# Channel mixing on one core: the first product by Strassen's scheme for four of six token blocks, with the weights' parts kept in DRAM

## The chip, the cores and the metric

The kernel runs on one core of a Trainium2 chip, in float32 values from end to end, where each value that a matmul takes is cut into two fp32r parts. The metric is the device time of one execution in microseconds (us). A profile of one execution is read beside it. Its engines are PE (TensorE, the matmuls), DVE (VectorE), ACT (ScalarE), POOL (GpSimd) and SP (which issues the DMAs here).

## The reference, cut to what matters

Three layers follow one another: attention with pooled queries, a mixture of four small attention experts, and a mixer. The change lies in the last lines, the channel mixing.

```python
def _moe2_ref(x, U, V, w_ch1, w_ch2):
    xt = x.transpose(0, 2, 1)
    h = xt @ U @ V
    u = x + h.transpose(0, 2, 1)                       # 4 x 576 x 512
    ch = np.maximum(u @ w_ch1, 0.0) @ w_ch2            # 512 -> 2048 -> 512
    return (u + ch).astype(np.float32)
```

## The kernel before, in words

The first 730 us belong to attention, the experts and the token mixing; they leave `u` in DRAM (`u_d`, 2304 tokens of 512 features). Channel mixing then takes six **token blocks** x of 384 tokens. The 2048 hidden features are 16 **slices** fi of 128. A slice has a tile `w` with its part of both weights, each of them as a high and a low half in fp32r.

For one block and one slice, `mlp(x, fi)` does this. `up` runs 12 matmuls of 128x384 into a PSUM bank `ms` (L1096): four chunks of 128 features, and for each high times high, high times low, low times high. ACT writes `hh`, the ReLU in fp32r (L1099), and DVE writes what is left over, `hl` (L1100). `down` runs 9 matmuls of 128x512 into the block's three banks `o` (L1107), and is called one step late: the `down` of the step before stands behind the `up` of this one, so that ACT and DVE have the length of a `down` for `hh` and `hl`. I call one such step a **tick**.

Slices go in `NG = 4` groups of `FG = 4`: within a group all six blocks are done, each over the group's four slices, and then DVE adds `o` to the block's `u` (`close_block`, L1112, three adds). There are 24 such closings. The order is `order = [(x, fi) for g ... for x ... for fi ...]`. Block 0 with the first group runs already among the experts' work (`CM`).

Weights arrive as float64. `weights` loads one tile of 128x512 as pairs of int32 (`raw`, 512 KB). `decode_steps` makes float32 of them in six DVE instructions (L241 to L246, tiles `dca` and `dcb`), and `cut` splits the result: ACT copies the high half (L224), and DVE, or POOL for the first group, subtracts it for the low half (L225). Of the 32 tiles the first eight are made during the experts' work. The other 24 are made by `ahead`, half a tile per tick, over three of the four groups.

`turn` transposes a block's `u`: three PE transposes (L1088) into a bank `ms`, then `cut` into `uh` and `ul`. The order of the instructions on PE, DVE and ACT is written out by hand:

```python
        if pend:
            finish()
        pend.append((x, fi, hl, ob[x]))
```

PSUM has three banks for `ms`, and the `o` of an odd block takes one of them (`OB`).

## Time and profile before

| | before |
|---|---|
| time, median of 3 runs | 1136.07 us (1135.33 to 1137.54) |
| profiled execution, its own time | 1135.58 us |
| span of that execution in the profile | 1133.6 us |
| PE busy over the span | 1099.6 us (97%) |
| DVE, ACT, POOL busy | 753.6, 456.1, 499.9 us |
| read from DRAM, written | 52.65 MB, 9.44 MB |

The profile is of one execution, whose own time is 1.98 us over its span. Busy shares are means over the whole span; the stage of the change is its last 400 us, where POOL has nothing to do and PE hardly ever waits.

### The profile page before, as it was taken

The numbers are of one execution on the slowest core, as the hardware profiler recorded it, in microseconds if no ns is written. First come the engines' busy times: TensorE is split into PE (matmuls) and PEld (weight loads), VectorE is DVE, ScalarE is ACT, GpSimd is POOL, SyncE is SP. The second block draws the span as 40 slices with busy tenths as digits, with TensorE's granted clock in tenths as the row PEclk, the third lists the DMA queues.
The fourth block names the chain that finished last, engine by engine and source line by source line (L and its number), as shares of the span: only waits on it lengthen the run. The fifth ranks groups of instructions, "written<-read, shape, count | busy, mean of one in ns | idle before, by whom it ended". The sixth has DMA issues, their size and how long they took to land.

```text
span 1133.6 us, 18983 instructions
## 1 busy us (share of the span) xinstructions
PE 1099.6 (97%) x6748; PEld 905.9 (80%) x6748; DVE 753.6 (66%) x1625; ACT 456.1 (40%) x1173; POOL 499.9 (44%) x492
## 2 busy tenths in 40 slices
...
POOL 6788999888888889844243334200000000000000
...
GB/s 143 193 177 187 183 199 173 170 175 198 176 173 157 179 142 90 43 43 43 43 43 85 38 170 103 143 129 56 57 19 32 61 56 1 56 56 5 53 56 56
DMA packets 115118, 117.96 MB, mean 104 GB/s; under 512 B 70352, under 2 KB 86736, under 8 KB 115024
## 3 DMA queue, kind: packets, MB, share of 16 engines
...
q8 instruction: 53, 0.87, 0.3%
q14 instruction: 41, 0.34, 0.1%
HBM read 52.65 MB, written 9.44 MB: 55 GB/s over the span
## 4 chain that ended last, share of the span: by engine, by line
PE 87%; DVE 7%; ACT 2%; issue 1%; DMA 1%; POOL 0%; POOLq 0%; ACTq 0%; SPq 0%
PE ms L1096 17%; PE o L1107 17%; PE pv L624 12%; PE ms L743 9%; PE st L604 8%; PE ms L556 7%; PE st L605 6%; PE pv L894 2%; PE ms L631 2%; DVE mp L558 2%; PE ms L504 1%; PE ms L815 1%; PE st L870 1%; PE st L869 1%; PE pv L946 1%
## 5 line engine op out<-in xcount | busy, mean ns | idle before, releaser
L616 POOL TENSOR_TENSOR acc<-acc,pt 128x576 f32<-128x576 f32 x224 | 319.5, 1427 | 34.0 <-ACT pt L606 19.5
L606 ACT ACTIVATE pt<-st 128x288 f32<-128x288 f32 x576 | 219.6, 409 | 187.8 <-PE st L605 140.7
L558 DVE TENSOR_REDUCE mp<-ms 128x1 f32<-128x384 f32 x432 | 215.1, 549 | 57.5 <-PE ms L556 55.5
L1096 PE MATMUL ms<-uh,w 128*128 128x384 f32 x768 | 214.4, 340 | 1.0 <-DVE ul L225 1.0
L1107 PE MATMUL o<-w,hh 128*128 128x512 f32 x576 | 180.9, 395 | 2.5 <-ACT hh L1099 2.2
L1100 DVE SCALAR_TENSOR_TENSOR hl<-ms,hh 128x384 fp32r<-128x384 f32 x96 | 53.5, 558 | 186.4 <-ACT hh L1099 185.9
L1099 ACT ACTIVATE hh<-ms 128x384 fp32r<-128x384 f32 x96 | 47.2, 491 | 273.7 <-PE ms L1096 273.7
L624 PE MATMUL pv<-pt,vr 128*64 128x288 f32 x1152 | 153.9, 412 | 0.0
L556 PE MATMUL ms<-kn,bd 128*128 128x384 f32 x432 | 146.3, 365 | 3.3 <-DVE mp L558 1.5
L1096 PEld LDWEIGHTS ms<-uh,w 128*128 128x128 f32 x768 | 141.0, 188 | 4.9 <-DVE ul L225 0.9
L1096 PE MATMUL ms<-ul,w 128*128 128x384 f32 x384 | 130.1, 339 | 0.7 <-DVE ul L225 0.7
L624 PEld LDWEIGHTS pv<-pt,vr 128*64 128x64 f32 x1152 | 80.8, 138 | 56.3 <-issue 5.2
L1107 PEld LDWEIGHTS o<-w,hh 128*128 128x128 f32 x576 | 107.0, 188 | 20.5 <-ACT hh L1099 2.5
L1107 PE MATMUL o<-w,hl 128*128 128x512 f32 x288 | 113.6, 394 | 0.0
L604 PE MATMUL st<-q1a,s1a 128*128 128x288 f32 x288 | 93.6, 325 | 2.2 <-ACT pt L606 2.0
L604 PE MATMUL st<-q1b,s1b 128*128 128x288 f32 x288 | 92.5, 321 | 0.2 <-ACT pt L606 0.2
L556 PEld LDWEIGHTS ms<-kn,bd 128*128 128x128 f32 x432 | 81.0, 194 | 14.0 <-DVE mp L558 5.8
L605 PE MATMUL st<-q2a,s2a 128*128 128x288 f32 x288 | 85.3, 296 | 0.0
L605 PE MATMUL st<-q2b,s2b 128*128 128x288 f32 x288 | 85.0, 295 | 0.0
L1096 PEld LDWEIGHTS ms<-ul,w 128*128 128x128 f32 x384 | 72.2, 188 | 5.3 <-DVE ul L225 1.9
L604 PEld LDWEIGHTS st<-q1a,s1a 128*128 128x128 f32 x288 | 54.4, 189 | 24.7 <-issue 21.2
L886 POOL TENSOR_TENSOR acc<-acc,pt 128x576 f32<-128x576 f32 (+4 forms) x48 | 45.9, 956 | 50.2 <-ACT pt L877 48.3
...
## 6 DMA issues: line engine op xcount, KB each, us to landing
...
```

The source lines that it names most:

```text
L556: nc.tensor.matmul(ps[:, :384], BD[i % 2][:, t, :], KN[i % 2][:, c * 384:c * 384 + 384], start=True, stop=True)
L558: nc.vector.tensor_reduce(st["mp"][:, t, c:c + 1], ps[:, :384], axis=X, op=ALU.max)
L604: nc.tensor.matmul(ps[:, :HT], pr.S1[a][:, ks], pr.Q1[a][:, qs], start=True, stop=False)
L605: nc.tensor.matmul(ps[:, :HT], pr.S2[a][:, ks], pr.Q2[a][:, qs], start=False, stop=True)
L606: nc.scalar.activation(c["pt"][:, a, :], ps[:, :HT], AF.Exp, scale=0.0625)
L616: nc.gpsimd.tensor_add(acc[i, h], acc[i, h], c["pt"])
L624: nc.tensor.matmul(o[64 * a:64 * a + 64, :HT], vr[:, a, kt, :], c["pt"][:, a, :], start=(kt == 0), stop=(kt == NKT - 1))
L743: nc.tensor.matmul(ps, stat[x][s], mov[x][m], start=(x == 0 and y == 0), stop=(x == n - 1 and y == 2))
L1096: nc.tensor.matmul(ps[:, :TB], W[fi][:, 0, a, cs], m[:, c, :], start=(c == 0 and y == 0), stop=(c == NC - 1 and y == 2))
L1099: nc.scalar.activation(h, ps[:, :TB], AF.Relu)
L1100: nc.vector.scalar_tensor_tensor(l, ps[:, :TB], 0.0, f(h), op0=ALU.max, op1=ALU.subtract)
L1107: nc.tensor.matmul(o[s_], hl[m][:, r], W[fi][:, 1, a, :], start=(fi % FG == 0 and y == 0), stop=(fi % FG == FG - 1 and y == 2))
```

## The change

Blocks 0 and 1 go on as before, slice by slice, but now through all 16 slices at once, so that each of their `o` stays in PSUM to the end. This part is the **base**: 28 ticks, first (1, 0) to (1, 3), then blocks 1's and 0's other slices in turn. In it all 24 remaining weight tiles are decoded, one in each of its first 24 ticks. The first of the six decode instructions is now an ACT instruction (Abs, L1065); the low half's subtraction stays on DVE (now L227), one tick later. Each decoded tile of float32 is written to DRAM (`keep`, into `v_d`, 256 KB).

Then come two passes over all slices: **pass 1** for blocks 2 and 3, **pass 2** for blocks 4 and 5. A pass has eight **units** `seven(p, k)`, each for two blocks and the two slices 2k and 2k+1. The first product is taken as a product of 2x2 blocks (two token blocks, two halves of the 512 features, two slices) by Strassen's seven products in place of eight. A product has 6 matmuls of 128x384 (L1268). DVE and ACT put the four results together from the seven (L1277, L1280), then make `hh` and `hl` of them as before, and `down` follows for each of the four (L1218).

The seven products need sums of the operands. For the moving side `lift` transposes a quarter of the two blocks' `u` and ACT copies it (L1173); `blend` adds such quarters (L1191) and cuts the sum; the combinations `bc` serve a whole pass. For the stationary side `combine` adds two pieces of the weights on POOL (L1123, tile `tw`) and cuts the sum (ACT and POOL, tile `cb`, 128x256); this is done in pass 1 only, for each unit anew, from a fetch of the decoded weights (`fetch_v`, 1 MB). What it makes is written to DRAM (`w_d`, seven times 256 KB per unit) and pass 2 reads it back (`fetch`). The second weight is read from `v_d` in both passes and cut again (`second`).

The other jobs stand in a table by tick (`at`), and `more()` runs those of a tick; a unit has four. POOL's and SP's order is now written out by hand too in this part. Each `o` is summed over all 16 slices, so that there are 18 adds at the end of blocks in place of 72.

```diff
-LATE = 7
+LATE = 0
...
+    w_d = udram.tile([FF // P // 2 * 2, P, 4 * DM], F32, name="w_d")
+    v_d = udram.tile([FF // P // 2, P, 4 * DM], F32, name="v_d")
...
+        def steps():
+            if x == 0:
+                W[fi] = w_slot(fi).tile([P, 2, 2, DM], F32R, name="w")
+            w = W[fi]
             if wide:
                 a = ct["dec"].tile([P, NC * P], I32, name="dca", bufs=1)
-                gs, v_ = decode_steps(r.rearrange("p c n w -> p (c n) w"), a,
-                                      ct["dec"].tile([P, NC * P], I32, name="dcb"), nc.vector)
+                b = ct["dec"].tile([P, NC * P], I32, name="dcb") if fi < NW else \
+                    ct["e"].tile([P, NC * P], I32, name="dce", tag="e")
+                y = r.rearrange("p c n w -> p (c n) w")
+                gs, v_ = decode_steps(y, a, b, nc.vector)
+                if fi >= NW:
+                    gs[0] = lambda: nc.scalar.activation(f(a), f(y[:, :, 1]), AF.Abs) and None
             else:
                 gs, v_ = [], r.rearrange("p c n -> p (c n)")
-            return gs + [lambda: cut(v_, w[:, x, 0], w[:, x, 1], eng)]
+            V1[fi, x] = v_
+            return gs, lambda: cut(v_, w[:, x, 0], w[:, x, 1], nc.vector if fi >= NW else nc.gpsimd)
...
+    def keep(fi, x):
+        y = 2 * x + fi % 2
+        nc.sync.dma_start(v_d[fi // 2][:, y * DM:(y + 1) * DM], V1.pop((fi, x)))
...
-    def ahead(g, x, k):
-
-        p = (x - 2) * FG + k
-        if g + 1 == NG or p < -1 or p >= FG * FG:
-            return
-        if p % 2 == 0:
-            todo.extend(nxt.pop()())
-        for y in [todo.pop(0) for _ in range((len(todo) + 1) // 2 if p % 2 == 0 else len(todo))]:
-            y()
...
+    PIECES = ["m5", "m3", "m1", "m2", "m4", "m6", "m7"]
+    SUMS = {"m1": (0, 3, ALU.add), "m2": (2, 3, ALU.add), "m5": (0, 1, ALU.add),
+            "m6": (2, 0, ALU.subtract), "m7": (1, 3, ALU.subtract)}
+
+    def place_of(k, m):
+        n = PIECES.index(m)
+        return w_d[2 * k + n // 4][:, n % 4 * 2 * HD2:(n % 4 + 1) * 2 * HD2]
...
+    def fetch_v(k):
+        UNIT[1, k] = ct["cw1"].tile([P, 4 * DM], F32, name="wv", tag="w")
+        nc.sync.dma_start(UNIT[1, k], v_d[k])
...
+    def fetch(k, r):
+        t = ct["cw0" if r else "cw1"].tile([P, 4 * DM], F32R, name="w")
+        ms = PIECES[4 * r:4 * r + 4]
+        nc.sync.dma_start(f(t[:, :len(ms) * DM]), w_d[2 * k + r][:, :len(ms) * DM])
+        for y, m in enumerate(ms):
+            PART[2, k, m] = t[:, y * DM:(y + 1) * DM]
...
+    def second(p, k, y, eng):
+        if y == 0:
+            t = ct["cw0"].tile([P, 4 * DM], F32R, name="w")
+            PART[p, k, "w2"] = [[t[:, (2 * z + a) * DM:(2 * z + a + 1) * DM] for a in range(2)] for z in range(2)]
+        cut(UNIT[1, k][:, (2 + y) * DM:(3 + y) * DM] if p == 1 else UNIT[2, k, y], *PART[p, k, "w2"][y], eng)
...
+    def combine(k, m):
+        v_ = UNIT[1, k][:, :2 * DM].rearrange("p (q n) -> p q n", q=4)
+        if m in SUMS:
+            x, y, op = SUMS[m]
+            t = ct["t"].tile([P, HD2], F32, name="tw", bufs=3)
+            nc.gpsimd.tensor_tensor(t, v_[:, x], v_[:, y], op=op)
+        else:
+            t = v_[:, 0 if m == "m3" else 3]
+
+        def rest():
+            if m in SUMS:
+                q = cbs[0] % 6
+                cbs[0] += 1
+                cb = ct["dec"].tile([P, 2 * HD2], F32R, name="cb", tag="dca", bufs=1) if q == 3 else \
+                    ct["dec"].tile([P, 2 * HD2], F32R, name="cb", tag="dcb") if q > 3 else \
+                    ct["e"].tile([P, 2 * HD2], F32R, name="cb", tag="e")
+            else:
+                z = k % 2 * 2 + (m == "m4")
+                if z == 0:
+                    UNIT["a"] = ct["cw0"].tile([P, 4 * DM], F32R, name="w")
+                cb = UNIT["a"][:, z * DM:(z + 1) * DM]
+            PART[1, k, m] = cb
+            cut(t, cb[:, :HD2], cb[:, HD2:], nc.gpsimd)
+            return lambda: nc.sync.dma_start(place_of(k, m), f(cb)) and None
+
+        return rest
...
+    def lift(p, ci, d):
+
+        x, h = QUAD[d]
+        if d == 0:
+            STG[p, ci] = ct["bc"].tile([P, 4, TB], F32, name="sg", tag="bc") if p == 1 and ci else \
+                xpool.tile([P, 4, TB], F32, name="sg", tag="x")
+        nc.scalar.activation(STG[p, ci][:, d], turn_(2 * p + x, h * HC + ci), AF.Copy)
...
+    def blend(p, ci, m, eng):
+        if ci == 0:
+            n = PIECES.index(m)
+            q = ct["bc"] if p == 1 or n == 6 else ct["u0"] if n < 3 else xpool
+            kw = {} if q is ct["bc"] else {"tag": "y" if q is ct["u0"] else "x"}
+            MOVE[p, m] = q.tile([P, 2, HC, TB], F32R, name="bc", **kw)
+        d, sg = MOVE[p, m], STG[p, ci]
+        if len(MOVES[m]) == 1:
+            t = sg[:, MOVES[m][0]]
+        else:
+            tn[0] += 1
+            if p == 1 and tn[0] % 2:
+                t = SPARE[0][:, tn[0] // 2 % 2]
+            else:
+                t = ct["t"].tile([P, TB], F32, name="tb")
+            x, y, op = MOVES[m]
+            eng.tensor_tensor(t, sg[:, x], sg[:, y], op=op)
+        return lambda: cut(t, d[:, 0, ci], d[:, 1, ci], eng)
...
-                nc.tensor.matmul(o[s_], hl[m][:, r], W[fi][:, 1, a, :],
-                                 start=(fi % FG == 0 and y == 0), stop=(fi % FG == FG - 1 and y == 2))
-
-    def close_block(x, g, o):
-        for s_ in range(NS):
-            nc.vector.tensor_add(U[x][:, s_, :], o[s_], U[x][:, s_, :])
...
+    def spread_h(src):
+        n = hn[0] = hn[0] + 1
+        if n % 4 < 2:
+            h, l = ct["wk"].tile([P, TB], F32R, name="hh"), ct["wk"].tile([P, TB], F32R, name="hl")
+        else:
+            y = ct["stg"].tile([P, 2, TB], F32R, name="hs", tag="raw")
+            h, l = y[:, 0], y[:, 1]
+        nc.scalar.activation(h, src, AF.Relu)
+        nc.vector.scalar_tensor_tensor(l, src, 0.0, f(h), op0=ALU.max, op1=ALU.subtract)
+        return h, l
...
+    def seven(p, k, late, more):
+
+        x0, x1 = 2 * p, 2 * p + 1
+        w2 = PART[p, k, "w2"]
+        s = {}
+
+        def mul(m):
+            w = PART[p, k, m]
+            ps = pms.tile([P, 512], F32, name="ms")
+            b = MOVE[p, m]
+            for c in range(HC):
+                for y, (i, j) in enumerate(((0, 0), (0, 1), (1, 0))):
+                    nc.tensor.matmul(ps[:, :TB], w[:, i * HD2 + c * P:i * HD2 + c * P + P], b[:, j, c, :],
+                                     start=(c == 0 and y == 0), stop=(c == HC - 1 and y == 2))
+            s[m] = ps[:, :TB]
...
+        mul("m5")
+        copy("m5")
+        if late:
+            down(*late.pop(0))
+        more()
+        mul("m3")
+        copy("m3")
+        add("c12", "m3", "m5s")
+        mul("m1")
+        add("c22", "m1", "m3s")
+        add("c11", "m1", "m5s", ALU.subtract)
+        h12 = spread_h(s["c12"])
+        if late:
+            down(*late.pop(0))
+        close()
+        more()
+        mul("m2")
+        copy("m2")
+        add("c22", "c22", "m2", ALU.subtract)
+        mul("m4")
+        add("c21", "m4", "m2s")
+        add("c11", "c11", "m4")
+        h21 = spread_h(s["c21"])
+        down(x1, 2 * k, h12, w2[0])
+        more()
+        mul("m6")
+        add("c22", "c22", "m6")
+        h22 = spread_h(s["c22"])
+        mul("m7")
+        add("c11", "c11", "m7")
+        h11 = spread_h(s["c11"])
+        down(x0, 2 * k + 1, h21, w2[1])
+        more()
+        late.extend([(x1, 2 * k + 1, h22, w2[1]), (x0, 2 * k, h11, w2[0])])
...
+    base = [(1, fi) for fi in range(n)] + [(x, fi) for fi in range(n, NF) for x in range(2)]
...
+    def decode(m):
+        gs, end = raws.pop(m)()
+        for g in gs:
+            g()
+        keep(n + m // 2, m % 2)
+        return lambda: end() and None
...
+    T1 = len(base)
+    T2 = T1 + 4 * NK
+    for m in range(2 * (NF - n)):
+        at(max(LATE if 2 <= m <= 17 else 0, m + LATE - (2 if m > 19 else 4)), lambda m=m: fetch_raw(m))
+        at(m + LATE, lambda m=m: decode(m))
+    for x in (2, 3):
+        at(T1 - 24 + 4 * x, lambda x=x: load_u(x))
+        at(T1 + 4 * NK - 4, lambda x=x: load_u(x))
+    for x in (4, 5):
+        at(T1 + 1, lambda x=x: load_u(x))
+        at(T2 + 8, lambda x=x: load_u(x))
+    for y in range(8):
+        at(T1 - 11 + y // 2, lambda y=y: lift(1, y // 4, y % 4))
+        at(T1 + 4 + y + 10 * (y // 4), lambda y=y: lift(2, y // 4, y % 4))
+    for y in range(14):
+        m, ci = PIECES[y // 2], y % 2
+        at(T1 - 7 + y if y < 3 else T1 - 4 + (y - 3) // 3,
+           lambda y=y, m=m, ci=ci: blend(1, ci, m, nc.gpsimd if y % 3 == 1 else nc.vector))
+        at(T1 + 8 + y + 7 * (y // 7), lambda y=y, m=PIECES[y % 7]: blend(2, y // 7, m, nc.gpsimd))
+    for k in range(NK):
+        s1, s2 = T1 + 4 * k, T2 + 4 * k
+        for y, m in enumerate(PIECES):
+            at(s1 - 5 + y * 4 // 7, lambda k=k, m=m: combine(k, m))
+        for y in range(2):
+            at(s1 - 2 + y, lambda k=k, y=y: second(1, k, y, nc.vector))
+            at(s2 - 5, lambda k=k, y=y: fetch_2(k, y))
+            at(s2 - 2 + y, lambda k=k, y=y: second(2, k, y, nc.vector))
+            at(s2 - 6 + y, lambda k=k, y=y: fetch(k, y))
+        at(s1 - 8 if k > 1 else T1 - 9 + 2 * k, lambda k=k: fetch_v(k))
...
+        for t, (x, fi) in enumerate(base):
+            if t == LATE:
+                open_late()
             mlp(x, fi)
-        open_late()
-        for y in range(2, NB):
-            load_u(y)
-        for x, fi in order[max(n, LATE):]:
-            mlp(x, fi)
-        finish()
+            close()
+            more()
+        down(*pend.pop())
+        late = []
+        for p in (1, 2):
+            for k in range(NK):
+                seven(p, k, late, more)
```

Three places show what moved. First DVE in the decoding of weights. Before, two ticks of the first group, where `hl` marks the tick:

```order
L1100 SCALAR_TENSOR_TENSOR hl<-ms,hh 128x384
L241 TENSOR_SCALAR dca<-raw 128x512
L242 TENSOR_SCALAR dca<-dca 128x512
L243 TENSOR_SCALAR dca<-dca 128x512
L244 TENSOR_SCALAR dcb<-raw 128x512
L225 TENSOR_TENSOR ul_9952<-ms,uh_9951 128x384
L1100 SCALAR_TENSOR_TENSOR hl<-ms,hh 128x384
L245 SCALAR_TENSOR_TENSOR dcb<-dca,dcb 128x512
L246 SCALAR_TENSOR_TENSOR dcb<-raw,dcb 128x512
L225 TENSOR_TENSOR w<-dcb,w 128x512
```

Now a whole tile stands in one tick of the base; L1203 writes `hl`, and L244 to L248 are the old L242 to L246:

```order
L1203 SCALAR_TENSOR_TENSOR hl<-ms,hh 128x384
L227 TENSOR_TENSOR w<-dce,w 128x512
L244 TENSOR_SCALAR dca<-dca 128x512
L245 TENSOR_SCALAR dca<-dca 128x512
L246 TENSOR_SCALAR dce<-raw 128x512
L247 SCALAR_TENSOR_TENSOR dce<-dca,dce 128x512
L248 SCALAR_TENSOR_TENSOR dce<-raw,dce 128x512
L1203 SCALAR_TENSOR_TENSOR hl<-ms,hh 128x384
```

The subtraction behind each `hl` is that of the tile decoded one tick before, and no half tiles are left.

Second PE in the first unit of pass 1, from its first product to its second `down` of its own. `bc` and `cb` are the combinations, `w` an uncombined piece, `hs` an `hh` or `hl` in another buffer:

```order
L1268 MATMUL ms<-bc,cb 128x384 x6
L1268 MATMUL ms<-bc,w 128x384 x6
L1268 MATMUL ms<-bc,cb 128x384 x12
L1268 MATMUL ms<-bc,w 128x384 x6
L1218 MATMUL o_0_11182<-w,hh 128x512 x2
L1218 MATMUL o_0_11182<-w,hl 128x512
L1218 MATMUL o_1_11183<-w,hh 128x512 x2
L1218 MATMUL o_1_11183<-w,hl 128x512
L1218 MATMUL o_2_11184<-w,hh 128x512 x2
L1218 MATMUL o_2_11184<-w,hl 128x512
L1268 MATMUL ms<-bc,cb 128x384 x12
```

This unit has no `down` of a unit before it between its products, so that five products (30 matmuls) stand one behind the other; before, every 12 matmuls of an `up` were followed by 9 of a `down`.

Third POOL around the start of pass 1. Before, its last work is the low halves of the first group's weights:

```order
L225 TENSOR_TENSOR w<-dcb,w 128x512
L886 TENSOR_TENSOR acc<-acc,pt 128x2x192
L886 TENSOR_TENSOR acc<-acc,pt 64x2x64
L225 TENSOR_TENSOR w<-dcb,w 128x512 x6
L1185 UNCONDITIONAL_BRANCH
```

Now these are followed by the blends of pass 1 (`bc`, and L1191 for the sums) mixed with the combinations of unit 0 (`tw`, `cb`, `w`), and then by those of the units behind it:

```order
L227 TENSOR_TENSOR w<-dcb,w 128x512 x6
L227 TENSOR_TENSOR bc<-sg,bc 128x384
L1123 TENSOR_TENSOR tw<-wv 128x256
L227 TENSOR_TENSOR cb<-tw,cb 128x256
L227 TENSOR_TENSOR w<-wv,w 128x256
L1191 TENSOR_TENSOR u_9512<-sg 128x384
L1123 TENSOR_TENSOR tw<-wv 128x256 x2
L227 TENSOR_TENSOR bc<-u_9512,bc 128x384
L227 TENSOR_TENSOR cb<-tw,cb 128x256 x2
```

A queue that was empty from here on has 12 instructions of 128x256 for each unit of pass 1, and in two runs of seven ticks a blend per tick beside them.

## Rows read from the trace of the kernel before

**Rows 1.** The page: span, busy time by engine, POOL over 40 slices.

```profile
span 1133.6 us, 18983 instructions
PE 1099.6 (97%) x6748; PEld 905.9 (80%) x6748; DVE 753.6 (66%) x1625; ACT 456.1 (40%) x1173; POOL 499.9 (44%) x492
...
POOL 6788999888888889844243334200000000000000
```

**Rows 2.** Stretch, its length, then PE, PEld, DVE, ACT, POOL busy, PEclk, DMA share, GB/s.

```profile
735.00:800.00 65.00, 62.89 (x330) 55.78 (x329) 38.38 (x74) 15.73 (x32) 0.00 (x0) 1.00 0.27 91
...
900.00:1000.00 100.00, 100.00 (x502) 90.68 (x501) 51.59 (x97) 16.73 (x32) 0.00 (x0) 1.00 0.14 43
```

**Rows 3.** PE in order of time: start, length, instructions, [idle before <-releaser].

```profile
900.67 0.34 PE L1096 MATMUL ms<-uh,w 128*128 128x384 f32 x1
...
902.78 0.63 PE L1107 MATMUL o<-w,hh 128*128 128x512 f32 x2
...
904.88 0.34 PE L1096 MATMUL ms<-uh,w 128*128 128x384 f32 x1
```

**Rows 4.** PE in order of time where four turns stand together.

```profile
748.89 0.82 PE L1088 MATMUL ms<-ident,u 128*128 128x128 f32 x6
...
750.61 1.01 PE L1088 MATMUL ms<-ident,u 128*128 128x128 f32 x6 [0.90 <-DVE ul L225]
...
752.33 0.44 PE L1096 MATMUL ms<-uh,w 128*128 128x384 f32 x1 [0.71 <-DVE ul L225]
```

**Rows 5.** Groups by shape, 560 to 1134 us: busy, mean ns | idle before.

```profile
L1100 DVE SCALAR_TENSOR_TENSOR hl<-ms,hh 128x384 fp32r<-128x384 f32 x96 | 53.5, 558 | 186.4 <-ACT hh L1099 185.9
L1099 ACT ACTIVATE hh<-ms 128x384 fp32r<-128x384 f32 x96 | 47.2, 491 | 273.7 <-PE ms L1096 273.7
L1112 DVE TENSOR_TENSOR u<-o,u 128x512 f32<-128x512 f32 x72 | 45.5, 683 | 1.8 <-PE o L1107 1.7
...
L245 DVE SCALAR_TENSOR_TENSOR dcb<-dca,dcb 128x512 int32<-128x512 int32 x32 | 21.8, 682 | 0.0
L224 ACT ACTIVATE w<-dcb 128x512 fp32r<-128x512 f32 x32 | 20.2, 633 | 50.6 <-DVE dcb L246 50.5
L225 DVE TENSOR_TENSOR w<-dcb,w 128x512 fp32r<-128x512 f32 x24 | 16.6, 693 | 16.9 <-ACT w L224 16.9
```

**Rows 6.** DVE in order of time: the parts of two decodes.

```profile
765.33 0.43 DVE L242 TENSOR_SCALAR dca<-dca 128x512 f32<-128x512 f32 x1
...
766.13 0.42 DVE L244 TENSOR_SCALAR dcb<-raw 128x512 int32<-128x512 int32 x1
...
788.01 0.68 DVE L245 SCALAR_TENSOR_TENSOR dcb<-dca,dcb 128x512 int32<-128x512 int32 x1
788.72 0.69 DVE L246 SCALAR_TENSOR_TENSOR dcb<-raw,dcb 128x512 int32<-128x512 int32 x1
790.11 0.69 DVE L225 TENSOR_TENSOR w<-dcb,w 128x512 fp32r<-128x512 f32 x1 [0.70 <-ACT w L224]
```

**Rows 7.** POOL and DVE in order of time, four places.

```profile
120.76 0.73 POOL L225 TENSOR_TENSOR wqk<-stg,wqk 128x256 fp32r<-128x256 f32 x1
...
127.56 1.44 POOL L225 TENSOR_TENSOR wqk<-stg,wqk 128x256 fp32r<-128x256 f32 x1
...
127.41 0.99 DVE L497 TENSOR_TENSOR qp<-qr 96x768 f32<-96x768 f32 x1
...
685.18 0.86 POOL L886 TENSOR_TENSOR acc<-acc,pt 128x320 f32<-128x320 f32 x1 [0.79 <-ACT pt L877]
...
685.31 1.28 DVE L246 SCALAR_TENSOR_TENSOR dcb<-raw,dcb 128x512 int32<-128x512 int32 x1
...
699.64 1.74 POOL L886 TENSOR_TENSOR acc<-acc,pt 128x384 f32<-128x384 f32 x2 [3.89 <-ACT pt L877]
```

**Rows 8.** Stretches again, for the DMA columns at the end of the line.

```profile
740.00:743.00 3.00, 3.00 (x17) 2.84 (x16) 0.00 (x0) 0.20 (x1) 0.00 (x0) 1.00 1.01 362
...
100.00:200.00 100.00, 98.80 (x699) 76.03 (x697) 74.12 (x166) 59.31 (x175) 91.99 (x72) 1.00 0.82 185
```

More of the change, by code (lines that the diff above doesn't have):

```diff
@@ L1057, in split @@
     def split(fi):
[L1058 to L1076 removed]
+        for x, g in enumerate([weights(fi, x) for x in range(2)]):
+            gs, end = g()
+            for y in gs:
+                y()
+            end()
+            keep(fi, x)
@@ new lines @@
+    cbs = [0]
+    def combine(k, m):
[22 more added lines that the diff above has]
+        return rest
@@ L1101, in up, with down @@
         return h, l
-    def down(x, fi, hl, o):
+    ob = {}
+    OB = [[(pst, "st")] * 3, [(ppv, "pv")] * 2 + [(pms, "ms")]]
+    def down(x, fi, hl, w2):
+        if x not in ob:
+            ob[x] = [q.tile([P, DM], F32, name=f"o{x}_{s_}", tag=t) for s_, (q, t) in enumerate(OB[x % 2])]
+            ob[x, "n"] = 0
+        n = ob[x, "n"]
+        ob[x, "n"] += 1
         for s_ in range(NS):
@@ L1118 @@
-    OB = [[(pst, "st")] * 3, [(ppv, "pv")] * 2 + [(pms, "ms")]]
-    order = [(x, fi) for g in range(NG) for x in range(NB) for fi in range(g * FG, g * FG + FG)]
-    ob, pend = {}, []
-    def finish():
-        x, fi, hl, o = pend.pop()
-        down(x, fi, hl, o)
-        if fi % FG == FG - 1:
-            close_block(x, fi // FG, o)
+                nc.tensor.matmul(ob[x][s_], hl[m][:, r], w2[a], start=(n == 0 and y == 0),
+                                 stop=(n == NF - 1 and y == 2))
+            if n == NF - 1:
+                closing.append((x, s_))
@@ L1128, in mlp, with close @@
+    closing = []
+    def close():
+        while closing:
+            x, s_ = closing.pop(0)
+            nc.vector.tensor_add(U[x][:, s_, :], ob[x][s_], U[x][:, s_, :])
+            nc.sync.dma_start(out_t[x * TB + s_ * P:x * TB + s_ * P + P, :], U[x][:, s_, :])
+    pend = []
     def mlp(x, fi):
-        g = fi // FG
-        if fi % FG == 0:
-            ob[x] = [p.tile([P, DM], F32, name=f"o{x}_{g}_{s_}", tag=t)
-                     for s_, (p, t) in enumerate(OB[x % 2])]
         hl = up(x, fi)
-        ahead(g, x, fi % FG)
@@ L1149, with at @@
     n = len(CM)
-    with tc.manual_schedule(engines=by_hand):
-        for x, fi in order[n:LATE]:
-            mlp(x, fi)
-        open_late()
-        for y in range(2, NB):
-            load_u(y)
-        for x, fi in order[max(n, LATE):]:
-            mlp(x, fi)
-        finish()
+    NK = NF // 2
+    base = [(1, fi) for fi in range(n)] + [(x, fi) for fi in range(n, NF) for x in range(2)]
+    todo, late_ = {}, {}
+    def at(t, g):
+        todo.setdefault(t, []).append(g)
+    tick = [0]
```

117 lines of the change are left out of this document (72 added, 45 removed).

## The prediction

> **What bounds the kernel now.** I read the page first: PE is busy for 97% of a span of 1133.6 us, and POOL's row of slices is empty from about 735 us on [rows 1]. Then the stretches of channel mixing: from 900 to 1000 us PE is busy 100.00 of 100 us at full granted clock, DVE 51.6, ACT 16.7, POOL 0, and the DMA engines 0.14 of their time [rows 2]. So the end is set by the number of matmuls and their pitch, and by nothing else. Last I read PE in order of time. An `up` begins at 900.67, its `down`'s place at 902.78, the next `up` at 904.88 [rows 3]. That gives 2.11 us for 12 matmuls of 128x384, 0.1758 us each, and 2.10 us for 9 of 128x512, 0.2333 us each. A tick is 4.21 us. The durations of single matmuls in the trace overlap and are of no use here; the starts are. The only stretch with idle PE is 735 to 800, 2.1 us of 65 [rows 2]. There four turns stand together: from 748.89 to 752.33 they take 3.44 us, with waits of 0.90 and 0.71 us for DVE's `ul` [rows 4].
>
> The sum is made against the profiled execution's own 1135.58 us (its span and 1.98 us around it), which is 0.5 us under the median of 1136.07. A difference of about 0.2% (2.3 us) is what a measurement of this kernel can tell from no change.
>
> **What is removed.** Sixteen units have 7 products of 6 matmuls where 8 stood: 96 matmuls fewer, at 0.1758 us, are **16.9 us** of PE [rows 3]. A unit should take 42 x 0.1758 + 36 x 0.2333 = 15.8 us in place of 16.8. The 54 closing adds that go (0.683 us each [rows 5]) lie on DVE, which is idle half the time: nothing. All this is given back only where the operands of the products are there in time; so the question is what the other engines do per tick.
>
> **The base: decoding a tile per tick.** DVE has per tick `hl`, five decode instructions and one subtraction. By starts, the old L242 to L243 and on to L244 take 0.80 us (765.33 to 766.13), L245 0.71, L244 and L246 about as long as their 0.42 and 0.69 [rows 6], `hl` and the subtraction 0.56 and 0.69 [rows 5]: 3.9 us of 4.21. The chain from tile to tile is: L246's end, ACT's high half 0.70 us later (the wait at 790.11 [rows 6]), ACT's Abs, then the five decode instructions of 2.6 us. Abs has no row; the nearest are ACT's 128x512 copy at 0.63 us [rows 5] and, for the bitwise step that it replaces, L244, which reads `raw` like it and takes 0.42 [rows 6]. At 0.63 the lap is 3.9 to 4.0 us, under a tick: **0 us**. The cover is thin. If Abs took twice as long, the lap would be 4.6 us, and 24 ticks would lose 0.4 us each, 9 us. I keep 0 and 9 as ends, and lean to 0, since reading `raw` costs DVE nothing extra.
>
> **Turns and lifts.** Before, 3.44 us stood where 12 transposes alone need about 1.0 (0.24 for three by the pitch of 0.82 for six, with what the matmul behind gains [rows 4]): 2.4 us of stall, which goes. In its place four ticks of the base have two lifts each. The second one and the next `up` need a bank that ACT's copy of the lift frees; I take 0.6 us per tick from the same two waits (1.61 us for four turns), **2.4 us**, so that the two cancel, and 0 to 4 as ends. The eight lifts of pass 1 stand one per tick between products.
>
> **Start of pass 1.** In the last five ticks of the base (21 us) DVE and POOL make the 14 blends and unit 0's parts. On POOL these are twelve instructions of 128x256, 0.73 us [rows 7], 8.8 us, and about nine of 128x384, about 0.87 (two took 1.74 [rows 7]), 8 us. On DVE there are 15 instructions of 128x384 with two SBUF inputs (0.683 at 512 elements [rows 5], so 0.52), four subtractions and four last decode steps: 13.5 us, beside 5 `hl`. If they only lie side by side, POOL has 17 of 21 us and the start costs the waits of five products in a row in two free banks, about **2 us**. If instructions of DVE with two SBUF inputs and those of POOL exclude each other, 30 us of work stand in 21 us.
>
> That they do is shown by rows of before. POOL's subtraction of 128x256 takes 0.73 us at 120.76 and 1.44 at 127.56, where DVE's 0.99 us with two SBUF inputs began at 127.41. DVE's L246 of 0.69 us takes 1.28 at 685.31, where POOL ran from 685.18 to 686.04 [rows 6, 7]. By the rows the later one of a pair waits for the earlier one.
>
> The Trainium skill, "SBUF — State Buffer", section "Who interferes with whom", has it as a rule: DVE's second pair of SBUF ports is GpSimd's only pair, and it is locked exclusively. It speaks against this change, which gives POOL work for 130 us beside a DVE with two-input instructions; the trace agrees (1.44 for 0.73 us), and with the lock the sum is 1127.7 us, without it 1122.2.
>
> Of the 9 us too many about half is hidden, since unit 0's last parts are wanted 8 us after its first: I take **4.5 us**, with 2 and 9 as ends.
>
> **POOL in pass 1.** A unit's parts are 12 instructions on POOL, 8.8 us of 15.8, and DVE's four `hl` from SBUF and two subtractions are 3.6 us with two SBUF inputs: 12.4 us by turns, which fits. In two runs of seven ticks (27.6 us) the blends for pass 2 stand on POOL too: 12 instructions of 128x384, about 0.95 us, 11 us. With 15.4 for the parts and 6.3 on DVE that is 33 us, 5 too many. Parts are made a unit ahead, which gives some 4 us. So each run costs 1 to 2 us, **3 us** for both; 0 if there is no exclusion (26.7 of 27.6 us), 10 if nothing is hidden.
>
> **DMA.** A unit of pass 1 moves 1 MB in and 1.8 MB out, about 180 GB/s; pass 2 about 146. Before, 362 GB/s went at a share of 1.01 in 740 to 743, when the blocks' `u` came in pieces of 768 KB, and 185 at 0.82 in the attention, with its many small transfers [rows 8]. The transfers here are 256 KB and more, nearer to the former, so I take 0. Fetches stand 5 to 8 ticks ahead of use, 20 to 33 us. SP's queue is in order, and a write waits in it for its cut, with the fetches behind it; at the start of the base, the load of the second `raw` pair stands behind a `keep`: **0.5 us**. The start of pass 2 (other operands, all made long before) and the end: **0.5 us**. The end itself is as now, two `down`s with their closing adds behind the last `hl`.
>
> **Sum.** 1135.58 - 16.9 + 0 + 0 + 4.5 + 3 + 1 = 1127.2; with 0.5 for the median, **1127.7 us**.
>
> **Rivals.**
> 1. *No exclusion that matters* (the start 2, the runs 0, the rest 1): 1135.58 - 16.9 + 3 + 0.5 = 1122.2, with lifts at 0 down to 1120. For it: POOL's two adds at 699.64 kept 0.87 us each beside DVE [rows 7]. Against it: the two lengthened rows. Chance 0.27.
> 2. *POOL falls behind through all of pass 1, slower than before.* POOL is alone with the parts, and every instruction of it that meets DVE's takes 1.44 in place of 0.73 us [rows 7]. Twelve of them are 17.3 us per unit, 1.5 over the 15.8 that PE needs. It decides from a mean of 1.32 us: below that, units outside the runs wait for nothing. At 1.44 pass 1 loses 12 us, each run 7 more (its 12 wider ones at 0.6 us each), the start 9: 1136.07 - 16.9 + 12 + 14 + 9 + 1 = 1155; half of it is 1137. Against it: DVE has only 3.6 us of such instructions per unit, too few to meet all twelve. Chance 0.13.
> 3. *The base's lap is over its tick.* Abs at 1.2 us: +9 on the forecast, 1137; the gain is gone from a lap of 4.55 us. Chance 0.10.
> 4. *DMA sets pass 1.* If what goes out moved no faster than the attention's 185 GB/s at 0.82, a unit of 2.84 MB would take 15.4 us, just under 15.8; with 10% less, +1.3 us per unit, 1138. Chance 0.05.
>
> **How the numbers follow.** The forecast (1124 to 1133) has 0.45. It and rival 1 are faster by over 0.2% (under 1133.8), and so is a tenth of the rest: 0.74. Rivals 2 to 4 at their small ends lie within 0.2%: 0.12. Their large ends are slower: 0.14. For 8 in 10 the range begins at rival 1's 1120 and ends at 1138, the middle of rivals 2 to 4; the forecast's own is 1124 to 1133.
>
> **What would show it.** Right: PE's products (L1268) are 672 at a pitch of 0.176 us, units of pass 2 take 15.8 us, and PE's idle time stands in three places, at the start of pass 1 and in the two runs of blends, put down to POOL's `cb` or ACT's high half behind it. POOL's 128x256 instructions have a mean between 0.8 and 1.1 us. In the base `hl` follows `hh` without delay, and ticks last 4.21 us but for the lifts. Wrong: ticks of 4.4 us and more all through the base (rival 3), units of pass 1 all of one length over 16.5 us with POOL busy without a gap (rival 2) or a DMA share near 1 (rival 4), or no idle time at all in pass 1 (rival 1). What I see least well is how a delay on one queue passes to the others, since DVE, ACT, POOL and SP are all in order now and wait for each other in each tick.

## The result, and the profile after

The changed kernel takes 1123.67 us (median of 4 runs, 1122.36 to 1127.36) against 1135.7 us for the kernel before: a ratio of 0.9897, with a 95% interval from 0.9870 to 0.9924. That is 12 us faster, where 8.4 were forecast. The profiled execution took 1122.36 us, with a span of 1120.6.

The page of the profile after, in the lines that answer to [rows 1]:

```profile
span 1120.6 us, 19602 instructions
PE 1081.5 (97%) x6652; PEld 887.4 (79%) x6652; DVE 812.8 (73%) x1707; ACT 542.3 (48%) x1361; POOL 614.2 (55%) x620
...
POOL 6888999988888888854424243200009596800000
```

There are 6652 matmuls in place of 6748: the 96 of the sum. POOL has work again in slices that were empty, and only there, from about 835 to 985 us. PE's waits behind the start of the base (735 us to the end), all of them:

```profile
PE ms L1268 <- DVE c L1280: 3.7, 2, 3.2
PE ms L1199 <- ACT sg L1173: 1.0, 4, 0.3
PE o L1218 <- DVE hl L1203: 0.9, 1, 0.9
```

The columns are the total in us, the number of waits and the longest. In stretches, for [rows 2] (the start of pass 1, the rest of pass 1, most of pass 2, and two us right behind the long wait):

```profile
850.00:885.00 35.00, 30.84 (x149) 27.51 (x148) 25.70 (x38) 16.40 (x39) 28.23 (x31) 0.95 0.76 269
885.00:985.00 100.00, 99.45 (x502) 88.84 (x501) 54.50 (x87) 49.22 (x114) 75.94 (x88) 1.00 0.55 186
985.00:1110.00 125.00, 125.00 (x625) 112.82 (x625) 62.23 (x118) 36.45 (x71) 0.00 (x0) 1.00 0.44 155
...
864.00:866.00 2.00, 2.00 (x8) 2.00 (x7) 2.00 (x5) 0.54 (x2) 2.00 (x3) 0.51 0.72 303
```

PE still sets the pace everywhere but at the start of pass 1. Behind its wait of 3.2 us the granted clock is at 0.51, which is about the lower of its two levels (1.2 of 2.4 GHz), so that the wait is paid for once more. PE in order of time, for [rows 3, 4]: the anchor that is used below, two ticks with lifts, the start of pass 1, the first product of its second unit, and the same place in two units of pass 2:

```profile
733.97 0.50 PE L1218 MATMUL o<-w,hh 128*128 128x512 f32 x1 [0.25 <-POOL w L227]
...
808.23 0.45 PE L1199 MATMUL ms<-uh,w 128*128 128x384 f32 x1 [0.25 <-ACT sg L1173]
...
813.61 0.44 PE L1199 MATMUL ms<-uh,w 128*128 128x384 f32 x1 [0.26 <-ACT sg L1173]
...
855.34 0.50 PE L1218 MATMUL o<-w,hl 128*128 128x512 f32 x1 [0.93 <-DVE hl L1203]
...
857.08 1.21 PE L1268 MATMUL ms<-bc,cb 128*128 128x384 f32 x6
858.12 1.23 PE L1268 MATMUL ms<-bc,w 128*128 128x384 f32 x6
859.19 1.21 PE L1268 MATMUL ms<-bc,cb 128*128 128x384 f32 x6
863.63 1.97 PE L1268 MATMUL ms<-bc,cb 128*128 128x384 f32 x6 [3.24 <-DVE c L1280]
...
873.66 1.23 PE L1268 MATMUL ms<-bc,cb 128*128 128x384 f32 x6
...
1003.05 1.21 PE L1268 MATMUL ms<-bc,w 128*128 128x384 f32 x6
...
1018.69 1.21 PE L1268 MATMUL ms<-bc,w 128*128 128x384 f32 x6
```

A unit of pass 2 takes 15.64 us (1003.05 to 1018.69). A tick with two lifts takes 5.38 us.

The time of attention and the experts, which the change hardly touches, differs by up to 5.6 us from one execution to the next (the row at 733.97 stands between 733.3 and 738.9 in the traces below). So the traces are compared by what lies **behind the anchor**: from the first `down` of the base, the one that waits 0.25 us for POOL's `w`, to the end of the span. Before, the same `down` stands at 734.33, so that this is 1133.6 - 734.33 = 399.3 us; after, 1120.6 - 733.97 = **386.6**, 12.6 less.

| kernel | median us | ratio to before, 95% | behind the anchor, us |
|---|---|---|---|
| before | 1135.7 | | 399.3 |
| changed | 1123.67 | 0.9897 (0.9870 to 0.9924) | 386.6 |
| e1 seventh product twice | 1141.32 | 1.0036 (1.0021 to 1.0050) | 402.2 |
| e2 last `down` later | 1123.45 | 0.9882 (0.9864 to 0.9900) | 386.7 |
| e3 POOL's blends earlier | 1124.16 | 0.9890 (0.9863 to 0.9916) | 385.9 |
| e4 first decode step on DVE | 1133.51 | 0.9961 (0.9940 to 0.9981) | 393.6 |
| e5 POOL's sums twice | 1146.13, one run | | 406.3 |
| e6 parts written twice | 1128.29, one run | | 387.6 |
| e8 blends of pass 1 on DVE | 1121.25 | 0.9863 (0.9844 to 0.9882) | 383.6 |
| e9 and a lighter start | 1123.66 | 0.9885 (0.9866 to 0.9906) | 385.5 |
| e10 e8, e2 and a blend later | 1120.48 | 0.9862 (0.9848 to 0.9877) | 384.3 |
| e11 parts on DVE from unit 2 | 1126.37 | 0.9909 (0.9894 to 0.9924) | 388.3 |
| e12 changed kernel again | 1125.2 | 0.9896 (0.9879 to 0.9914) | 386.5 |

### The profile page after: what moved, and what is told of

The parts are those of the page before. It is cut to its first block, busy times and chain, and to the rows that moved or that the text cites. A ratio compares the mean times of both kernels' runs of the same rounds, so it can differ in the third digit from the quotient of the medians.

```text
span 1120.6 us, 19602 instructions
## 1 busy us (share of the span) xinstructions
PE 1081.5 (97%) x6652; PEld 887.4 (79%) x6652; DVE 812.8 (73%) x1707; ACT 542.3 (48%) x1361; POOL 614.2 (55%) x620
## 4 chain that ended last, share of the span: by engine, by line
PE 82%; DVE 8%; POOL 4%; issue 2%; ACT 2%; DMA 2%; SPq 0%; POOLq 0%; ACTq 0%; DVEq 0%
PE o L1218 14%; PE pv L626 12%; PE ms L1268 9%; PE ms L745 9%; PE st L606 8%; PE ms L558 7%; PE st L607 6%; PE ms L1199 5%; PE pv L896 2%; PE ms L633 2%; DVE mp L560 1%; PE ms L506 1%; PE ms L817 1%; DVE xl L227 1%; PE st L872 1%
## 5 line engine op out<-in xcount | busy, mean ns | idle before, releaser
L1218 PE MATMUL o<-w,hh 128*128 128x512 f32 x384 | 120.2, 394 | 2.0 <-ACT hh L1202 1.7
L1268 PE MATMUL ms<-bc,w 128*128 128x384 f32 x432 | 84.7, 341 | 0.0
L1218 PEld LDWEIGHTS o<-w,hh 128*128 128x128 f32 x384 | 71.5, 188 | 13.9 <-ACT hh L1202 2.0
L1268 PEld LDWEIGHTS ms<-bc,w 128*128 128x128 f32 x432 | 77.6, 190 | 3.0
L1218 PE MATMUL o<-w,hl 128*128 128x512 f32 x192 | 75.5, 393 | 0.9 <-DVE hl L1203 0.9
L1199 PE MATMUL ms<-uh,w 128*128 128x384 f32 x256 | 71.8, 340 | 1.3 <-ACT sg L1173 1.0
L1218 PE MATMUL o<-w,hs 128*128 128x512 f32 x288 | 71.4, 392 | 0.0
L615 POOL TENSOR_TENSOR acc<-pt 128x576 f32<-128x576 f32 x32 | 50.7, 1586 | 34.8 <-ACT pt L608 34.8
L227 POOL TENSOR_TENSOR bc<-sg,bc 128x384 fp32r<-128x384 f32 x6 | 7.0, 1171 | 106.8 <-ACT bc L226 104.2
```

What stands on the lines that cost most here:

```text
L615: nc.gpsimd.tensor_add(t, acc[i, h], c["pt"])
L1199: nc.tensor.matmul(ps[:, :TB], W[fi][:, 0, a, cs], m[:, c, :], start=(c == 0 and y == 0), stop=(c == NC - 1 and y == 2))
L1218: nc.tensor.matmul(ob[x][s_], hl[m][:, r], w2[a], start=(n == 0 and y == 0), stop=(n == NF - 1 and y == 2))
L1268: nc.tensor.matmul(ps[:, :TB], w[:, i * HD2 + c * P:i * HD2 + c * P + P], b[:, j, c, :], start=(c == 0 and y == 0), stop=(c == HC - 1 and ...
```

## The experiments

My theory was that PE's matmuls set the time, and that what the change loses again lies at the start of pass 1, where POOL and DVE shut each other out of SBUF. The rivals: the order on PE (five products in a row, two free banks), DVE's own load, and DMA.

**e1, the removed work put back.** The product m7 is computed twice into the same bank.

```diff
-            for c in range(HC):
+            for c in (list(range(HC)) * 2 if m == "m7" else range(HC)):
```

> The seventh product of each unit is run twice, 6 more matmuls of 128x384 per unit, 96 in all, which takes back what Strassen's scheme removed on PE and leaves all else as it is. If PE's matmuls set the time of both passes (my theory), 96 x 0.1758 = 16.9 us come back: about 1123.7 + 16.9 = 1140.6, slower than before by some 4 to 5 us. If the units were held by POOL, DVE or DMA in places, the longer units would give these time, and less comes back: under 1135.

It took 1141.32 us, and 15.5 us more behind the anchor (402.2 for 386.6). So the two passes are bound by PE nearly throughout, and the rest of the change costs 402.2 - 399.3 = 2.9 us on balance. The 15.5 us are 1.4 less than the 16.9 put back: the longer units gave some time in pass 1 (the wait of 0.49 us that the changed kernel has ahead of its fifth unit is gone); the rest is not traced.

**e2, another order on PE at the start of pass 1.**

```diff
-        down(*pend.pop())
-        late = []
+        late = [pend.pop()]
```

> The last down of the base is put behind the first product of pass 1 in place of ahead of it. Rival theory (the order on PE: five products in a row with two free banks, and a down that waits 0.93 us for its hl): the 0.93 us go and the wait of 3.23 us shrinks by about 2, so 2.5 to 3 us faster, and the low granted clock behind it goes too, 1120 to 1121. My theory (the bank's copy m3s stands on ACT behind cuts that wait for POOL's late sums, so the fourth product begins at the same time whatever PE did before): the gap only changes place, 1123 to 1124.

386.7 us behind the anchor: nothing. The wait of 0.93 us went, and the long one grew from 3.24 to 3.68. What PE did ahead of the fourth product is not what it waited for.

What it waited for stands on the other three engines of the changed kernel, in order of time (POOL, then ACT, then DVE):

```profile
859.40 1.32 POOL L1191 TENSOR_TENSOR tb<-sg 128x384 f32<-128x384 f32 x1
860.68 1.17 POOL L1123 TENSOR_TENSOR tw<-wv 128x256 f32<-128x256 f32 x1
...
859.89 0.53 ACT L226 ACTIVATE bc<-u 128x384 fp32r<-128x384 f32 x1 [1.07 <-DVE u L1191]
860.75 0.52 ACT L226 ACTIVATE bc<-tb 128x384 fp32r<-128x384 f32 x1 [0.34 <-POOL tb L1191]
861.88 0.42 ACT L226 ACTIVATE cb<-tw 128x256 fp32r<-128x256 f32 x1 [0.61 <-POOL tw L1123]
862.21 0.40 ACT L226 ACTIVATE w<-wv 128x256 fp32r<-128x256 f32 x1
862.51 0.47 ACT L1277 ACTIVATE m3s<-ms 128x384 f32<-128x384 f32 x1
...
863.01 0.56 DVE L1280 TENSOR_TENSOR c<-ms,m5s 128x384 f32<-128x384 f32 x1 [0.75 <-ACT m3s L1277]
```

The bank for the fourth product is free when DVE has read the second one (863.01). Behind that stands ACT's copy `m3s`, whose product was done when the next one began (859.19 to 859.4) and which began at 862.51. ACT works in order, and of the cuts ahead of it the first (859.89) waited for a sum of DVE's, the next two for sums of POOL's. POOL is late, and so is DVE; in the 15 us ahead, neither had time left (DVE busy for 14.41 us, POOL for 15.00, the third and fifth of the busy times):

```profile
845.00:860.00 15.00, 14.07 (x71) 12.46 (x70) 14.41 (x19) 7.92 (x19) 15.00 (x15) 1.00 0.37 140
```

**e3, POOL's five blends of pass 1 ahead of the crowd,** in the ticks in which POOL idles and DVE decodes.

```diff
-        if ci == 0:
+        if (p, m) not in MOVE:
...
-        at(T1 - 7 + y if y < 3 else T1 - 4 + (y - 3) // 3,
+        at({1: T1 - 7, 4: T1 - 7, 7: T1 - 6, 10: T1 - 6, 13: T1 - 5}.get(y, T1 - 7 + y if y < 3 else T1 - 4 + (y - 3) // 3),
```

> The five of pass 1's fourteen blends that POOL makes are moved from the last four ticks of the base to the three ticks ahead of these, where POOL is idle and DVE decodes. My theory (POOL and DVE exclude each other and POOL is late at the start of pass 1): POOL is done with about 8 instructions of 1.0 to 1.3 us earlier, the wait of 3.23 us goes to under 1 and the low clock behind it goes, 3 to 5 us faster, 1119 to 1121; decode ticks with a blend get longer by up to 1 us where DVE's two-input instructions wait. Rival theory (order on PE, two banks): no change, 1123 to 1124. If the decode's cover is as thin as I put it, the three ticks lose 1 us each and take back most of the gain: 1122.

The long wait went (0.47 us are left), but 385.9 us behind the anchor is 0.7 less, and the median is no different. DVE's decode, POOL beside it, and what PE then waited for:

```profile
838.54 1.12 DVE L245 TENSOR_SCALAR dca<-dca 128x512 int32<-128x512 int32 x1
839.58 1.23 DVE L246 TENSOR_SCALAR dce<-raw 128x512 int32<-128x512 int32 x1
...
839.34 1.20 POOL L1191 TENSOR_TENSOR tb<-sg 128x384 f32<-128x384 f32 x1
...
849.99 0.50 PE L1218 MATMUL o<-w,hl 128*128 128x512 f32 x1 [1.90 <-DVE hl L1203]
```

Two steps of 0.42 us [rows 6] take 1.12 and 1.23 beside POOL, though they have one input, and 1.12 and 1.24 again in the next tick; DVE is then late with `hl`, and the wait has moved some 18 us ahead, low clock and all (0.80 and 0.77 in 848 to 856). The end of the expectation had this ("the three ticks take back most of the gain"); that instructions with one input are held up too, the prediction did not have.

**e4, the first decode step back on DVE.**

```diff
-                if fi >= NW:
-                    gs[0] = lambda: nc.scalar.activation(f(a), f(y[:, :, 1]), AF.Abs) and None
```

> The first decode instruction goes back from ACT to DVE, all else as it is. By the prediction's sum DVE then has 3.9 + 0.45 = 4.35 us of work in a tick of 4.21: 24 ticks lose about 0.15 us each, and more in the ticks with blends, 3 to 6 us slower, 1127 to 1130. If the cover in the base is wider than I worked out (DVE idle 0.4 us per tick in the trace), nothing: 1123 to 1124.

7 us slower behind the anchor, more than expected. ACT's cut of each decoded tile, one per tick:

```profile
803.11 0.63 ACT L226 ACTIVATE w<-dce 128x512 fp32r<-128x512 f32 x1 [3.43 <-DVE dce L248]
...
807.54 0.63 ACT L226 ACTIVATE w<-dce 128x512 fp32r<-128x512 f32 x1 [3.43 <-DVE dce L248]
...
811.99 0.63 ACT L226 ACTIVATE w<-dce 128x512 fp32r<-128x512 f32 x1 [3.43 <-DVE dce L248]
```

The lap is 4.44 us, over the tick of 4.20. The cover in the base is as thin as the prediction had it: 0.45 us of DVE work per tick turns it into the bound.

**e5, POOL loaded with more.** Each sum of a part is made twice.

```diff
             nc.gpsimd.tensor_tensor(t, v_[:, x], v_[:, y], op=op)
+            nc.gpsimd.tensor_tensor(t, v_[:, x], v_[:, y], op=op)
```

> Each of the five sums that POOL makes for a unit of pass 1 is made twice, about 0.85 us each by the trace, 4.2 us more of POOL per unit. POOL is busy 12.4 us of a unit's 15.8 in the profile after; with 16.6 it is over. If POOL's margin is what the trace shows, the six units behind the start lose about 0.8 us each and the start 2 to 4 more: 6 to 10 us slower, with PE waiting for cuts in every unit. If POOL's long instructions are stretched by waits that would be there anyway (the lock lets it catch up), under 3 us.

19.7 us slower behind the anchor, twice what I expected. PE's waits from 850 to 1000, and three stretches of pass 1 (ahead of the first run of blends, that run, and behind it):

```profile
PE ms L1269 <- DVE c L1281: 12.9, 8, 4.3
...
885.00:905.00 20.00, 19.36 (x101) 16.70 (x100) 9.64 (x15) 9.24 (x23) 15.48 (x20) 1.00 0.56 200
905.00:945.00 40.00, 34.62 (x169) 29.68 (x169) 19.43 (x28) 17.07 (x39) 38.85 (x45) 1.00 0.39 138
950.00:975.00 25.00, 23.99 (x119) 19.99 (x119) 13.66 (x21) 11.93 (x28) 21.01 (x27) 1.00 0.48 175
```

POOL is the bound in the run of blends, where it is busy for 38.85 of 40 us and PE for 34.62. Outside the runs, and behind the start, PE hardly waits, although POOL has 4.2 us more to do in each unit; the "cuts in every unit" of the expectation did not come. So POOL's margin in the changed kernel is thin in the runs and at the start, and wider between them. Over the whole stretch from 885 to 985 it is 24%, some 3.8 us of a unit.

**e6, DMA loaded with more.** Every part is written to two places.

```diff
+    x_d = udram.tile([FF // P // 2 * 2, P, 4 * DM], F32, name="x_d")
...
-    def place_of(k, m):
+    def place_of(k, m, far=0):
...
-            return lambda: nc.sync.dma_start(place_of(k, m), f(cb)) and None
+            return lambda: [nc.sync.dma_start(place_of(k, m, z), f(cb)) for z in range(2)] and None
```

> Each part of a unit is written to DRAM twice, to two places: 1.8 MB more per unit of pass 1, 4.6 MB in 15.8 us, about 290 GB/s where 362 GB/s went at a share of 1.01 before. The forecast's step (DMA hides with a margin): no change between the start of the base and the end, within 0.5 us, and the lengthened DVE and POOL instructions stay as they are, so DMA is not what stretches them. Rival (DMA takes part in the stretching or sits near its limit): units of pass 1 over 16.2 us, 3 us slower or more.

The rest of pass 1 then reads

```profile
885.00:985.00 100.00, 99.43 (x501) 88.54 (x501) 53.59 (x87) 49.57 (x115) 76.76 (x91) 1.00 0.88 300
```

with PE as busy at 300 GB/s as it was at 186. POOL's parts (0.851 and 0.878 us) have the same means as in the changed kernel, and DVE's `w<-wv` 1.061 us for 1.059. So neither the pace nor the stretching comes from DMA. Behind the anchor it is 0.9 us more, above the 0.5 that I had allowed. All of it lies in the first unit, which takes 17.62 us for 16.58 (862.00 to 879.62) behind the same wait (3.25): the granted clock in 850 to 885 is 0.90 for 0.95 there. Why it stayed lower is open.

**e8, all blends of pass 1 on DVE,** at the same ticks.

```diff
-           lambda y=y, m=m, ci=ci: blend(1, ci, m, nc.gpsimd if y % 3 == 1 else nc.vector))
+           lambda y=y, m=m, ci=ci: blend(1, ci, m, nc.vector))
```

> All blends of pass 1 are made on DVE, at the same ticks; POOL keeps only the parts of the units. The run with the early blends moved the wait instead of ending it: DVE's decode steps went from 0.43 to 1.1 and 1.2 us beside POOL. My theory (what the start of pass 1 costs is the time in which POOL and DVE exclude each other, whoever has the work): an instruction of 128x384 costs DVE 0.47 us from start to start and POOL 1.0, so 8 of them on DVE are about 4 us less of shared time, the wait of 3.23 us goes to under 1 and the low clock behind it goes, 3 to 5 us faster between the start of the base and the end. Rival (DVE is loaded to the brim there for itself and POOL's help is worth having): DVE gets 4 us more work in the last four ticks and the wait grows to 4 us or more, 1 to 3 us slower.

383.6 us behind the anchor, 3.0 less, and a median of 1121.25. The wait:

```profile
864.42 1.32 PE L1268 MATMUL ms<-bc,cb 128*128 128x384 f32 x6 [1.23 <-DVE c L1280]
```

and no low clock behind it (1.00 in 850 to 885). Giving DVE more work made the crowded stretch shorter, which excludes the rival (DVE loaded for itself). Whether POOL was late by the exclusion or by its own longer instructions, this run doesn't tell; e11 bears on that. 0.86 us for `hl` and 1.23 are left, more than the "under 1" expected.

**e9, three jobs put later on top of e8.**

```diff
-            at(s1 - 5 + y * 4 // 7, lambda k=k, m=m: combine(k, m))
+            at(s1 - (4 if k == 1 else 5) + y * 4 // 7, lambda k=k, m=m: combine(k, m))
...
-            at(s1 - 2 + y, lambda k=k, y=y: second(1, k, y, nc.vector))
+            at(s1 - (2 if k else 1) + y, lambda k=k, y=y: second(1, k, y, nc.vector))
...
-            close()
+            if t < T1 - 1:
+                close()
```

> As the run with the blends on DVE, and three jobs that the first products don't need are put later: unit 1's parts by a tick, unit 0's second weight by a tick, and block 0's closing adds into unit 0. My theory: what is left of the wait at the start of pass 1 goes, 4 to 6 us faster than the changed kernel between the start of the base and the end, 1118 to 1120. Rival (the wait is set by the order on PE): as the changed kernel, 1123 to 1124.

A miss: 385.5 us, 1.9 more than e8. Two new waits stand in it:

```profile
867.85 0.70 PE L1218 MATMUL o<-w,hh 128*128 128x512 f32 x2 [1.50 <-DVE u L1228]
...
880.37 1.31 PE L1268 MATMUL ms<-bc,cb 128*128 128x384 f32 x6 [1.52 <-ACT sg L1173]
```

Block 3's first `down` needs the banks that block 1's closing adds free, and these now stood behind block 0's; and unit 1's later cuts stood on ACT ahead of a lift.

**e10, e8 with the `down` of e2 and the two blends of m7 later.**

```diff
-        at(T1 - 7 + y if y < 3 else T1 - 4 + (y - 3) // 3,
+        at(T1 - 7 + y if y < 3 else T1 - 4 + (y - 3) // 3 if y < 12 else T1 + 1,
...
```

> All blends of pass 1 on DVE as in the run before last; the two of the seventh product, which is wanted last, two ticks later, so that ACT's copy of the second product no longer stands behind their cuts; and the last down of the base behind the first product, as in the second run. My theory (the shared time of POOL and DVE sets the start, and the order on ACT carries it to PE): of the 1.23 and 0.86 us that the run with DVE's blends still waits at the start of pass 1 at most 0.5 is left, 382 us from the first down of the base to the end against 383.6 and, for the changed kernel, 386.6: some 4 us faster than the changed kernel. If the copy is held by DVE's own load instead, the wait only moves: 383 to 384.

1120.48 us is the lowest median, and lower than the changed kernel on the same chip (e12: ratios 0.9862 and 0.9896, whose intervals do not meet). But behind the anchor it is 384.3, not the 382 expected and no better than e8, whose 383.6 and ratio (0.9863) it cannot be told from. ACT's copy is no longer late; DVE is:

```profile
859.79 1.21 DVE L227 TENSOR_TENSOR w<-wv,w 128x512 fp32r<-128x512 f32 x1
...
861.52 1.31 PE L1268 MATMUL ms<-bc,cb 128*128 128x384 f32 x6 [1.91 <-DVE c L1280]
```

The second branch of the expectation came true: the wait moved to DVE's queue, with instructions that are still stretched beside POOL's.

**e11, the parts of units 2 to 7 on DVE.**

```diff
-            nc.gpsimd.tensor_tensor(t, v_[:, x], v_[:, y], op=op)
+            (nc.vector if k > 1 else nc.gpsimd).tensor_tensor(t, v_[:, x], v_[:, y], op=op)
...
-            cut(t, cb[:, :HD2], cb[:, HD2:], nc.gpsimd)
+            cut(t, cb[:, :HD2], cb[:, HD2:], nc.vector if k > 1 else nc.gpsimd)
```

> From unit 2 on the parts are made on DVE (its sums and subtractions of 128x256), as they are on POOL in the changed kernel; POOL keeps the blends for pass 2. My theory (the stretching is POOL and DVE excluding each other): outside the two runs of blends DVE's subtraction of the second weight goes back from 1.06 to the 0.69 us that it takes in pass 2, and hl to 0.55; DVE has 12 x 0.35 = 4.2 us more per unit, 13 of 15.8, and the time stays within 1 us of the changed kernel's. Rival (the longer instructions come from DMA traffic or from ACT at the same tiles): they stay at 1.0 us without POOL.

The same DVE instruction without POOL and beside it, and POOL's blend:

```profile
955.33 0.69 DVE L227 TENSOR_TENSOR w<-wv,w 128x512 fp32r<-128x512 f32 x1
...
960.37 1.50 DVE L227 TENSOR_TENSOR w<-wv,w 128x512 fp32r<-128x512 f32 x1
...
960.13 1.20 POOL L1191 TENSOR_TENSOR tb<-sg 128x384 f32<-128x384 f32 x1
```

This settles the stretching: 0.69 us where POOL is silent, 1.50 where it runs. Between the two runs of blends, where POOL has nothing to do, `hl` takes 0.55 or 0.56 us throughout. The time was 1.7 us longer behind the anchor, against "within 1 us", with short waits of PE for DVE's `c`.

**e12, the changed kernel again.**

> The changed kernel once more, on the chip of the two others, so that they can be compared with it: 1122 to 1125, 386 to 387 us from the first down of the base to the end, a wait of about 3.2 us at the start of pass 1.

1125.2 us, 386.5 behind the anchor, a wait of 3.24: it repeats, and what lies behind the anchor is 0.2 us off in a second trace of the same kernel.

## Why the prediction was right, step by step

The time lies in the range of 1120 to 1138, and the way was right; but the likeliest time was 4 us too high, and the measured one stands just under the 1124 to 1133 that belong to the forecast. By the traces, against the terms of the sum:

- **Removed matmuls, 16.9.** A unit takes 15.64 us; it does the work of four ticks, 4.203 us each before (820.82 to 904.88 are 20 of them), so 16 x (16.81 - 15.64) = 18.7 us. The products give what was worked out; the rest, 0.1 us per unit, is that nine matmuls of a `down` take 2.07 (1004.09 to 1006.16) and not 2.10. Why is not known, so that these 1.8 us are luck. The first row is of before, the others of after:

```profile
820.82 0.34 PE L1096 MATMUL ms<-uh,w 128*128 128x384 f32 x1
...
1004.09 2.23 PE L1218 MATMUL o<-w,hs 128*128 128x512 f32 x9
1006.16 2.25 PE L1268 MATMUL ms<-bc,w 128*128 128x384 f32 x12
```

- **Start of pass 1, 4.5.** It cost about 6.0: the 0.93 us for `hl`, and a first unit of 16.58 us (857.08 to 873.66) whose 42 products and two `down`s need 11.5. Of these 5.1 us, 3.2 are the wait and nearly all of the rest the low clock behind it, which the prediction left out; without it the start would have cost about 4.3. The mechanism was right (POOL and DVE lengthen each other, by e11, and both are full there), with the detail that it reached PE by ACT's order. How much of the 6.0 is the exclusion alone, no run separates.
- **POOL in pass 1, 3.** This is the term that was most off. PE waited 0.5 us once in the two runs of blends. The prediction charged the whole of each collision to POOL; the trace shows it shared, as these groups of the changed kernel show (`cb` and `w<-wv` from the start of pass 1 on, with POOL at work; `w<-v` in pass 2 without):

```profile
L227 POOL TENSOR_TENSOR cb<-tw,cb 128x256 fp32r<-128x256 f32 x40 | 34.8, 878 | 17.4 <-ACT cb L226 17.4
...
L227 DVE TENSOR_TENSOR w<-wv,w 128x512 fp32r<-128x512 f32 x16 | 16.9, 1059 | 11.6 <-ACT w L226 11.6
...
L227 DVE TENSOR_TENSOR w<-v,w 128x512 fp32r<-128x512 f32 x16 | 11.1, 692 | 0.0
```

  POOL's 0.73 us became 0.88, DVE's 0.69 became 1.06, and DVE, half idle in pass 1, had that time. From 880 to 1000 us POOL's means are 0.83 us for the parts and 1.07 for the blends (0.95 was taken). By these, as an estimate, a run has 21 x 0.83 + 12 x 1.07 = 30 us of POOL in its 27.6 and not 33: under 3 too many, and the lead of the parts, put at 4 us, covers them. It was nearly used up even so: POOL runs without a gap for 13 us of the first run and for 14 of the second (the fifth of the busy times), and PE waits once, in the first:

```profile
911.00:924.00 13.00, 12.51 (x63) 10.98 (x62) 7.77 (x11) 5.75 (x13) 13.00 (x16) 1.00 0.63 205
961.00:975.00 14.00, 14.00 (x70) 12.47 (x69) 8.66 (x14) 7.70 (x18) 14.00 (x17) 1.00 0.56 197
...
922.67 1.34 PE L1268 MATMUL ms<-bc,cb 128*128 128x384 f32 x6 [0.49 <-DVE c L1280]
```

  With more work for POOL it is in these runs that PE waits (e5).
- **Turns and lifts, 0.** By difference (-12.6 = -18.7 + 6.0 + the rest) these and the wait of the runs cost 0.1 us on balance, against the 3 that the sum had for both together. Lifts cost about what turns had: 1.18 us for two in a tick.
- **Decode in the base, 0.** Right, with ticks of 4.20: ACT's Abs (L1065) takes 0.66 us, for the 0.63 taken. The price of the thin cover is e4's.
- **DMA and SP, 0.5, and start of pass 2, 0.5.** Nothing is to be seen of either: pass 2 waits nowhere, and e6 gives the margin.

So of the 4.2 us by which the traces lie under the sum, 1.8 are the units, 3.9 the terms for POOL's runs, the queue of SP and pass 2 that were too dear, and -1.5 the start. Of the three places named for PE's idle time two came out, the start and the first run. The measured time is nearer to rival 1's 1122.2 than to the forecast, but not by its mechanism: the exclusion is there (e11), and the start cost 6.0 us where rival 1 has 2. Of the others, e5 speaks against rival 2: even with 4.2 us more for POOL in each unit, units outside the runs hardly wait. e4 is rival 3 brought about, and e6 excludes rival 4.

The Trainium skill, "SBUF — State Buffer", section "Who interferes with whom", was the rule weighed. That two-input instructions of DVE and GpSimd shut each other out agrees with e11 (0.69 and 1.50 us). It also has copies and `tensor_scalar` of one input among those that can take the shared pair; e3 agrees (1.12 and 1.23 for 0.42 us), and the prediction had left this half out.
